# Later LayerNorm normalise behind a Newton pair, weight preparation after it, and residual loads moved to the end of the first gate/up pass

## The chip, the cores and the metric

The kernel runs on one core of one Trainium2 chip. The metric is the device time of an execution in microseconds (us); lower is better. Engines: PE is the matrix engine (PEld its weight loads), DVE the vector engine, ACT the scalar engine, POOL the GpSimd engine, SP the engine that only issues transfers here. All executions quoted are fast (mean granted matrix clock 0.990 to 1.000), and the ratios below compare times from the same chip and the same rounds; where medians of different rounds are set side by side, the text says so.

## The reference

```python
def reference(A_x, A_wqkv, A_wo, B_x, B_w_gate, B_w_up, B_w_down):
    x = A_x                                   # 1 x 2048 x 1024, bf16
    xn = _layernorm(x, axis=-1)               # eps 1e-5
    s = _A_ref(xn, A_wqkv, A_wo)              # linear attention, 32 heads of 32, phi = elu + 1
    g = _silu(_B_ref(xn, B_w_gate, B_w_up, B_w_down))   # silu(x Wg) * (x Wu), times Wd; F = 3584
    return x + s * g
```

So every token tile (128 tokens, 16 tiles) is normalised first, goes through the k/v projections and the k-v sums, later through q, the output projection and the large feed-forward part. At the end `x` and `s` are read again as residual inputs.

## The kernel before

Stage 1 handles 16 tiles `i` with four column pieces `c` each: `emit_Bmm` is 8 matmuls, `emit_Bev` evacuates them on ACT and DVE (`pk_sb` is DVE's result for pieces 0 and 1), and `emit_C(i-1)` adds the tile before to the k-v sums (`kvz`, needs `pk_sb`). Two pieces make a "half step". Behind this work the kernel prepares the statistics of tiles some steps ahead (`ln_pre`), normalises them (`emit_N`, whose result goes through a transposing transfer into `xnT`), and prepares feed-forward weights (`prep`: load, squared sum on ACT, scale on DVE, four subtractions on POOL, store).

```python
    PREP_AT = ((4, 3), (5, 3), (6, 1), (6, 3), (7, 3))
    # ... cut ...
    PRE_AT = {2: (5, 6), 3: (7, 8), 4: (9, 10), 5: (11, 12), 6: (13, 14), 7: (15,)}
    GRP = {5: (5, 6), 6: (5, 6), 7: (7, 8), 8: (7, 8), 9: (9, 10), 10: (9, 10), 11: (11, 12), 12: (11, 12),
           13: (13, 14), 14: (13, 14)}
    NR_ITERS = 3

    def emit_rstd(gid, eng=None):             # 1/sqrt(var + eps) of one or two tiles, by Newton's method
        eng = eng or nc.gpsimd
        mv, rstd, tiles = grp_state[gid]
        # ... cut: three small DVE instructions make the first guess y from a = var + eps ...
        for _ in range(NR_ITERS):
            eng.tensor_tensor(out=w[:, 0:n], in0=y, in1=y, op=ALU.mult)
            eng.tensor_tensor(out=w[:, 0:n], in0=w[:, 0:n], in1=a[:, 0:n], op=ALU.mult)
            eng.tensor_scalar(out=w[:, 0:n], in0=w[:, 0:n], scalar1=-0.5, scalar2=1.5, op0=ALU.mult, op1=ALU.add)
            eng.tensor_tensor(out=y, in0=y, in1=w[:, 0:n], op=ALU.mult)

    def ln_pre(i, eng=None):                  # statistics on DVE; Newton after the last tile of the group
        emit_stats(i)
        if i == grp_tiles(i)[-1]:
            emit_rstd(grp_of(i), eng)

    for i in range(2, NT):
        for c in range(NCH):
            # ... cut: statistics of wo and wv on ACT (so_stat), power-of-two scales ...
            if (i, c) != (2, 0):
                emit_Bmm(i, c)
            if c == 0:
                # ... cut ...
                emit_C(i - 1)
            emit_Bev(i, c)
            if (i, c) in PREP_AT:
                prep(1)
            if i >= 8 and c % 2 == 1:
                k = 2 * (i - 8) + c // 2
                prep(11 * (k + 1) // 16 - 11 * k // 16)
            if c % 2 == 1:
                for k in (PRE_AT[i - 1] if i - 1 in PRE_AT else (4,) if i == 2 else ())[c // 2:c // 2 + 1]:
                    emit_N(k)
                    # ... cut: loads of wo ...
                for k in PRE_AT.get(i, ())[c // 2:c // 2 + 1]:
                    ln_pre(k)
```

In the traces each engine's instructions start in the order written: in the kernel before, DVE stands 2.29 us for the normalise at 58.18 us, and the statistics written behind it start at 58.64. DVE meets, per tile: normalise, statistics, normalise, statistics, Newton's first guess, the phi work, and then the next normalise, which needs POOL's result of that Newton chain.

In the first of two gate/up passes (28 weight units, `n = 28`), some weights still arrive raw (`w_up`), and five pairs of residual tiles (128 KB of `x` and 128 KB of `s` each) are put on SP's issue queue. There the traces show one issue after the other: in the kernel before, one of `s` at 319.51 us takes 2.87 us, and the next one follows at 322.48. `io_load(mb)` makes each pair wait for the unit's matmul `mb`:

```python
                mb = emit_b(keys[i])
                if first and i in range(6, 11):
                    io_load(mb)
```

## Time and profile before

| | before |
|---|---|
| time, median of 4 executions | 765.71 us (764.83 to 766.57) |
| span of the profiled execution | 764.6 us |
| PE busy | 751.0 us (98%) |
| DVE, ACT, POOL busy | 73%, 49%, 36% |

Page of the kernel before: busy time of the engines, and the chain of work that ended last, by engine.

```profile
PE 751.0 (98%) x3731; PEld 349.3 (46%) x3731; DVE 556.3 (73%) x1043; ACT 376.2 (49%) x526; POOL 277.9 (36%) x340
...
PE 84%; DVE 6%; POOL 4%; DMA 3%; issue 2%; ACT 1%; SPq 0%; ACTq 0%; POOLq 0%
```

PE is nearly all of the span, but the chain that ended last is only 84% PE; the rest are stretches in which PE waited for something. Busy time in chosen 20-us stretches shows where: columns are the length, then busy us (instructions) of each engine, the granted clock, the share of the transfer engines and GB/s.

```profile
core 0: us, PE busy (x) PEld busy (x) DVE busy (x) ACT busy (x) POOL busy (x), PEclk, DMA share, GB/s
0.00:20.00 20.00, 17.33 (x84) 7.69 (x85) 14.31 (x53) 10.12 (x17) 0.80 (x9) 1.00 0.97 323
60.00:80.00 20.00, 17.18 (x99) 7.93 (x97) 15.03 (x43) 14.94 (x27) 8.04 (x27) 1.00 0.66 148
80.00:100.00 20.00, 17.93 (x111) 8.86 (x109) 15.86 (x35) 14.70 (x22) 19.09 (x22) 1.00 0.86 241
320.00:340.00 20.00, 18.65 (x89) 8.36 (x88) 15.10 (x28) 10.21 (x12) 10.23 (x12) 1.00 0.98 364
```

The start costs 2.7 us, stage 1 loses 2.8 and 2.1 us at 60 to 100 us, and 1.35 us are missing near 335 us. PE's waits name the releasers (total us, times, longest):

```profile
PE kvz L551 <- DVE pk_sb L163: 2.8, 4, 1.3
PE kv_ps L529 <- DVE pk_sb L163: 1.5, 1, 1.5
...
PE xb L940 <- ACT sg L1015: 1.2, 1, 1.2
PE kvz L551 <- ACT w_sb L260: 0.5, 1, 0.5
```

Now the chain of waits inside stage 1 (start us, duration, what). There is no PE in it: one turn leads from a normalise (L486) to the next one 8.93 us later.

```profile
49.25 0.55 DVE xn L486
49.80 1.21 DVE stats L448 x2
...
51.24 0.41 DVE xn L486
51.65 1.21 DVE stats L448 x2
...
53.12 0.18 DVE lna L470
...
54.15 0.73 POOL lnw L478
...
57.95 0.20 POOL rstd L481
58.18 0.55 DVE xn L486
```

DVE does two normalises, two statistics and the first guess, then POOL twelve operations on 128x2 elements (0.20 us each plus 0.07 us between them at best, up to 0.73 us for one, 4.4 us for all), and only then does the next normalise start. DVE stood 12.1 us for this in six waits between 36 and 95 us:

```profile
DVE xn L486 <- POOL rstd L481: 12.1, 6, 2.3
```

PE's own sequence in that time (start, duration, what, and in brackets the idle time just before and its releaser). The kvz groups come once per tile (in two halves of four where PE had to wait); the first two here are 7.36 us apart, the next 8.4, 8.9, 8.9:

```profile
48.06 0.63 PE L551 MATMUL kvz<-v_sb,pk_sb 128*128 128x129 bf16 x8
55.42 0.92 PE L551 MATMUL kvz<-v_sb,pk_sb 128*128 128x129 bf16 x8
...
63.80 0.40 PE L551 MATMUL kvz<-v_sb,pk_sb 128*128 128x129 bf16 x4 [0.55 <-DVE pk_sb L163]
...
72.72 0.40 PE L551 MATMUL kvz<-v_sb,pk_sb 128*128 128x129 bf16 x4 [0.32 <-DVE pk_sb L163]
...
81.59 0.39 PE L551 MATMUL kvz<-v_sb,pk_sb 128*128 128x129 bf16 x4
...
87.94 3.61 PE L529 MATMUL kv_ps<-wkv_sb,xnT 128*128 128x512 bf16 x16 [1.53 <-DVE pk_sb L163]
```

The stall near 335 us, in the chain of waits: a raw up-weight load issued at 317.05 lands 12.59 us later, ACT's work on it comes late, and PE waits for ACT.

```profile
317.05 12.59 DMA w_sb<-in_B_w_up_dram
...
332.32 1.89 ACT w_sb L1322
...
334.74 0.58 ACT sg L1015
...
335.36 1.02 PE xb L940 x4
```

### The profile page before, as it was taken

How to read it: one execution, taken by the hardware profiler on the slowest of the kernel's cores; microseconds unless marked ns; L12 is line 12 of the kernel's file. 1: busy time of each engine (PE TensorE's matmuls, PEld its weight loads, DVE VectorE, ACT ScalarE, POOL GpSimd, SP SyncE). 2: the span in 40 equal slices, each digit the busy share in tenths (PEclk: the TensorE clock that was granted, in tenths of full speed). 3: DMA queues.
4: the chain of work that ended last, by engine and by line, in shares of the span. 5: the costliest groups of instructions: out<-in, count | busy, mean ns of one | idle time of the engine just before them, and what ended most of it. 6: DMA issues, size and time to landing. Idle time of an engine off the chain costs nothing.

```text
span 764.6 us, 10494 instructions
## 1 busy us (share of the span) xinstructions
PE 751.0 (98%) x3731; PEld 349.3 (46%) x3731; DVE 556.3 (73%) x1043; ACT 376.2 (49%) x526; POOL 277.9 (36%) x340
## 2 busy tenths in 40 slices
PE   8998899999999999999999999999999999999997
PEld 3443444454444444444444444444444444444444
DVE  7767787888588788878889884458776767787335
ACT  4777666899865666566657411132323222211022
POOL 0443899998550255858686000110000000200000
PEclk9999999999999999999999999999999999999999
DMA  9966799959679669887889227398655444530824
GB/s 319 297 141 138 196 299 308 317 106 308 196 196 264 229 233 312 281 329 292 312 287 385 105 71 273 106 359 319 231 189 182 170 165 166 174 142 15 270 92 135
DMA packets 105845, 170.30 MB, mean 223 GB/s; under 512 B 34688, under 2 KB 82176, under 8 KB 95168
## 3 DMA queue, kind: packets, MB, share of 16 engines
q1 hardware_dynamic: 100144, 144.99, 58.5%
q0 software_dynamic: 4208, 22.15, 7.4%
q10 hardware_dynamic: 1440, 2.49, 1.1%
q8 instruction: 29, 0.48, 0.3%
q14 instruction: 24, 0.20, 0.1%
HBM read 111.67 MB, written 50.59 MB: 212 GB/s over the span
## 4 chain that ended last, share of the span: by engine, by line
PE 84%; DVE 6%; POOL 4%; DMA 3%; issue 2%; ACT 1%; SPq 0%; ACTq 0%; POOLq 0%
PE zw L940 23%; PE dzw L1125 12%; PE xb L940 12%; PE q_ps L183 7%; PE dx L1125 6%; PE yb L940 6%; PE kv_ps L529 6%; PE s_ps L749 3%; PE dy L1125 3%; PE fx L791 3%; DVE stats L448 2%; DMA w_sb<-in_B_w_up_dram 2%; POOL lnw L478 1%; DMA xp<-in_A_x_dram 1%; POOL rstd L481 1%
## 5 line engine op out<-in xcount | busy, mean ns | idle before, releaser
L940 PEld LDWEIGHTS <-w_sb 128*128 128x128 f16 (+1 forms) x1568 | 152.2, 98 | 184.4 <-issue 2.1
L529 PE MATMUL kv_ps<-wkv_sb,xnT 128*128 128x512 bf16 x512 | 113.9, 379 | 2.5 <-DVE pk_sb L163 1.5
L940 PE MATMUL xb<-xnT,w_sb 128*128 128x512 bf16 x448 | 115.0, 379 | 1.2 <-ACT sg L1015 1.2
L940 PE MATMUL zw<-xnT,w_sb 128*128 128x512 bf16 x448 | 105.8, 379 | 0.0
L940 PE MATMUL zw<-S,w_sb 128*128 128x512 f16 x448 | 105.8, 379 | 0.0
L295 POOL TENSOR_TENSOR w_sb<-w_sb 128x512 f16<-128x512 bf16 x42 | 50.6, 1204 | 94.3 <-DVE w_sb L283 51.6
L260 ACT ACTIVATE w_sb<-w_sb 128x2048 bf16<-128x2048 bf16 x42 | 79.9, 1902 | 9.6 <-DMA w_sb<-in_B_w_up_dram 9.6
L1125 PE MATMUL dx<-w_sb,hT 128*128 128x512 bf16 x210 | 79.6, 379 | 0.0
L529 PEld LDWEIGHTS <-xnT 128*128 128x128 bf16 x512 | 48.4, 98 | 58.5 <-issue 2.4
L1125 PEld LDWEIGHTS <-hT 128*128 128x128 bf16 (+1 forms) x462 | 45.2, 98 | 51.7
L183 PE MATMUL q_ps<-xnT,wq_sb 128*128 128x512 bf16 x256 | 58.4, 379 | 0.0
L1125 PE MATMUL dzw<-w_sb,hT 128*128 128x512 f16 x196 | 58.3, 379 | 0.0
L940 PE MATMUL yb<-S,w_sb 128*128 128x512 f16 x224 | 57.4, 378 | 0.0
L1016 ACT ACTIVATE sg<-cg 128x1024 bf16<-128x1024 f32 x28 | 29.6, 1057 | 56.4 <-DVE cg L1009 56.4
L1009 DVE SCALAR_TENSOR_TENSOR cg<-zw,rc_all,s 128x1024 f32<-128x1024 f32 x28 | 35.9, 1283 | 25.1 <-PE zw L940 14.0
L968 DVE SCALAR_TENSOR_TENSOR s<-yb,rc_all,s 128x512 f32<-128x512 f32 x42 | 31.5, 749 | 30.1 <-ACT s L967 30.1
L296 POOL TENSOR_TENSOR w_sb<-w_sb 128x512 f16<-128x512 bf16 x42 | 50.0, 1191 | 3.3
L298 POOL TENSOR_TENSOR w_sb<-w_sb 128x512 f16<-128x512 bf16 x42 | 50.7, 1208 | 0.0
L1065 POOL TENSOR_TENSOR hs<-hT 128x512 f16<-128x512 bf16 x2 | 2.5, 1252 | 132.6 <-ACT sg L1016 132.6
L297 POOL TENSOR_TENSOR w_sb<-w_sb 128x512 f16<-128x512 bf16 x42 | 50.3, 1199 | 0.0
L1099 POOL DMA_DIRECT2D out_dram<-io x16 | 8.7, 542 | 101.9 <-DVE io L1098 101.6
L967 ACT ACTIVATE s<-xb,rcl 128x512 f32<-128x512 f32 x14 | 9.6, 687 | 65.0 <-PE xb L940 65.0
(183 smaller groups left out, 1185.8 us busy)
## 6 DMA issues: line engine op xcount, KB each, us to landing
w_sb<-pk_g SPq DMA_DIRECT2D x27, 1024.0 KB, 5.7
pk_g<-w_sb SPq DMA_DIRECT2D x14, 1024.0 KB, 5.1
w_sb<-wd SPq DMA_DIRECT2D x14, 1024.0 KB, 5.4
w_sb<-pk_u SPq DMA_DIRECT2D x14, 1024.0 KB, 5.0
pk_u<-w_sb POOLq DMA_DIRECT2D x13, 1024.0 KB, 5.3
w_sb<-wd SPq DMA_DIRECT2D x14, 768.0 KB, 5.0
w_sb<-in_B_w_gate_dram SPq DMA_DIRECT2D x14, 512.0 KB, 5.5
w_sb<-in_B_w_down_dram SPq DMA_DIRECT2D x28, 256.0 KB, 5.0
```

The source lines that it names most:

```text
L183: nc.tensor.matmul(q_ps[:], lhsT=wq_sb[:, dc, g * P:(g + 1) * P], rhs=xn_ap(dc, btok), start=(dc == 0), stop=(dc == DC - 1))
L260: nc.scalar.activation(out=junk, in_=raw_view(key, t), func=ACT.Square, accum_out=asum[:])
L295: nc.gpsimd.tensor_tensor(out=T1, in0=b12, in1=b11, op=ALU.subtract)
L296: nc.gpsimd.tensor_tensor(out=T2, in0=b22, in1=T1, op=ALU.subtract)
L297: nc.gpsimd.tensor_tensor(out=T3, in0=b22, in1=b12, op=ALU.subtract)
L298: nc.gpsimd.tensor_tensor(out=T4, in0=b21, in1=T2, op=ALU.subtract)
L529: mm = nc.tensor.matmul(kv_ps[:], lhsT=xn_ap(dc, tok), rhs=wkv_sb[:, dc, c * CW:(c + 1) * CW], start=(dc == 0), stop=(dc == DC - 1))
L940: mm = nc.tensor.matmul(out, lhsT=lhs(k), rhs=rhs(k), start=(first and k == 0), stop=(k == HK - 1), skip_group_check=True)
L968: nc.vector.scalar_tensor_tensor(out=s2[:], in0=y_[:], scalar=rc, in1=s1[:], op0=ALU.mult, op1=ALU.add)
L1009: nc.vector.scalar_tensor_tensor(out=d12, in0=zw[:], scalar=rc, in1=s2[:, None, :].to_broadcast([P, 2, TB]), op0=ALU.mult, op1=ALU.add)
L1016: nc.scalar.activation(out=sg[:, 1:3, :], in_=cf[:], func=ACT.Silu)
L1125: nc.tensor.matmul(out, lhsT=lhs, rhs=rhs, start=first, stop=lastk, skip_group_check=True)
```

## The change

Its intent: each normalise of tiles 6 to 15 moves two half steps later, so that POOL's Newton result is ready when DVE gets there; the Newton pairs become (6,7), (8,9) ... (14,15), with tile 5 alone; weight preparation goes behind the normalise and loses one early slot, made up by 12 instead of 11 later; the residual loads go from units 6 to 10 to units 22 to 26 of the first pass.

```diff
-    PREP_AT = ((4, 3), (5, 3), (6, 1), (6, 3), (7, 3))
+    PREP_AT = ((4, 1), (5, 1), (6, 1), (7, 1))
@@
-        GRP = {5: (5, 6), 6: (5, 6), 7: (7, 8), 8: (7, 8), 9: (9, 10), 10: (9, 10), 11: (11, 12), 12: (11, 12),
-               13: (13, 14), 14: (13, 14)}
+        N_AT = {4: (4,), 6: (5,)}
+        for k in range(6, NT):
+            N_AT[k + 3] = (k,)
@@ def grp_tiles(gid):
-            return GRP.get(gid, (gid,))
+            return (gid,) if gid < 6 else (gid - gid % 2, gid - gid % 2 + 1)
@@ main loop of stage 1
                 emit_Bev(i, c)
-                if (i, c) in PREP_AT:
-                    prep(1)
-                if i >= 8 and c % 2 == 1:
-                    k = 2 * (i - 8) + c // 2
-                    prep(11 * (k + 1) // 16 - 11 * k // 16)
                 if c % 2 == 1:
-                    for k in (PRE_AT[i - 1] if i - 1 in PRE_AT else (4,) if i == 2 else ())[c // 2:c // 2 + 1]:
+                    for k in N_AT.get(2 * i + c // 2, ()):
                         emit_N(k)
                         # ... cut, unchanged ...
                     for k in PRE_AT.get(i, ())[c // 2:c // 2 + 1]:
                         ln_pre(k)
+                if (i, c) in PREP_AT:
+                    prep(1)
+                if i >= 8 and c % 2 == 1:
+                    k = 2 * (i - 8) + c // 2
+                    prep(12 * (k + 1) // 16 - 12 * k // 16)
@@ first gate/up pass
-                if first and i in range(6, 11):
+                if first and i in range(n - 6, n - 1):
                     io_load(mb)
```

## The prediction

> TensorE bounds the kernel: the page gives PE 751.0 of 764.6 us, so all its idle time is 13.6 us and no reordering can win over 1.8%. Busy time in 20-us stretches places it: 2.7 us at the start (untouched), 2.8 + 2.1 at 60 to 100 us, 0.5 near 223, 1.35 near 335, the rest at the end.
>
> **Stall 1, 60 to 88 us.** The table of waits shows PE waiting for DVE's pk_sb, 2.8 us in 4 waits before kvz and 1.5 once before kv_ps, and 0.5 for ACT. The chain of waits from 40 to 88 us has hardly any PE in it: DVE normalise (0.55), statistics of two tiles (2 x 1.2), Newton's head on DVE (0.6), twelve tiny POOL operations (4.4), the next normalise. One turn takes 8.93 us (49.25, 58.18, 67.09, 76.11), with DVE standing 2.3 us for POOL's last rstd; a tile costs PE about 7.4 us (32 matmuls 216 ns apart, kvz 0.46). This loop, not PE, paces tiles 4 to 8; until 60 us a backlog hides it.
>
> The change breaks the loop: the pair's Newton is started two or three half steps (over 7 us) ahead of the normalise, against 4.4 us of POOL. No operation is added: nine Newton chains before and after (tile 5 alone, 14 and 15 paired). Without the wait DVE has about 6.6 us per tile, under PE's 7.4. The 1.53 us at 86 us goes too: DVE waited there for tile 15's own Newton, then normalised in 1.35 instead of 0.55 us while POOL ran. [...] Transposes stay about 11 us ahead of their tile's first matmul, against 3.2 us to landing.
>
> Against it: preparation moves later, its squares onto tiles 7 to 9. There ACT has an estimated 7.7, 7.7 and 8.8 us per tile (2.1 per square, 1.25 per wo or wv square, 0.5 per piece) against PE's 7.4, so 0.3 to 1.5 us of stall may stay. POOL's T work starts one preparation later in program order, but near 79 us instead of 83.6, since DVE no longer lags; relative to PE nothing shifts. Gain: 4.9 less about 0.7, 4.2 us.
>
> **Stall 2, near 334 us.** The chain shows a raw w_up load issued at 317.05 landing after 12.59 us (median 5.4), then ACT's work on it, and PE waiting 1.2 us for ACT's sg. The issue queue interleaves five pairs of residual loads (256 KB each) between 295 and 322 us, with DMA about full; one holds the queue for 2.87 us. Moving them to units 22 to 26 (about 450 to 490 us, DMA share 0.3 to 0.7) takes 0.5 MB out of the way there, an estimated 1.5 us at the 350 GB/s seen, and the issue comes a microsecond earlier. Gain: 1.2 us. They are needed only after 515 us.
>
> Sum: 5.4 us off 766.55, so **761.2 us**; 80% range 758.5 to 765.0. Faster by over 2%: 1%; within 2%: 98%; slower by over 2%: 1%.
>
> **Right if:** PE busy stays near 751 and its idle time at 60 to 100 us is below 1.5 us; DVE no longer waits for POOL's rstd; the 8.93-us turn becomes about 7.4; that w_up load lands within 9 us and PE has no wait near 330.
>
> **Wrong if:** ACT on tiles 7 to 9 becomes the limit and gives back over 2 us; stores behind POOL hold the in-order issue queue, so that oT transposes near 150 us come late; another raw load stalls PE instead; late residual loads delay weight tiles of the first down pass.

## The result, and the profile after

The changed kernel takes 759.22 us (median of 4 executions, 759.13 to 759.30) against 765.71 us (764.83 to 766.57). The ratio is 0.9915, 95% interval 0.9898 to 0.9932; a ratio here is the mean time of one kernel's fast runs over that of the other's of the same rounds, so not quite the ratio of the medians. It is correct, and lies within 2% of before.

Page of the changed kernel, and its busy time in the three stretches that had lost time, columns as before (the lines of the file are one higher). This trace lacks 69 of PE's 3731 matmul records, so its PE busy time is too low by a few us, and full stretches read 19.89 instead of 20.00.

```profile
PE 746.2 (99%) x3662; PEld 349.2 (46%) x3731; DVE 559.9 (74%) x1043; ACT 375.7 (50%) x526; POOL 276.8 (37%) x340
...
PE 94%; DVE 2%; DMA 1%; ACT 1%; issue 1%; SPq 0%; ACTq 0%; DVEq 0%
```

```profile
60.00:80.00 20.00, 19.89 (x117) 9.92 (x118) 14.27 (x38) 16.56 (x30) 9.49 (x26) 1.00 0.77 133
80.00:100.00 20.00, 19.89 (x115) 9.74 (x116) 16.93 (x35) 15.52 (x23) 17.25 (x15) 1.00 0.84 277
320.00:340.00 20.00, 19.89 (x96) 9.10 (x97) 16.56 (x26) 11.38 (x15) 12.46 (x13) 1.00 0.83 294
```

The chain that ended last is now 94% PE, and the three stretches at 60 to 100 and at 320 to 340 us are full. PE's waits in the changed kernel (those left out are 0.4 us or less): neither pk_sb nor the feed-forward's sg is in the list.

```profile
PE warm_ps L566 <- DVE warm L563: 1.5, 1, 1.5
PE fx L792 <- DVE wq_sb L785: 0.5, 1, 0.5
...
PE nd L264 <- ACT w_sb L260: 0.3, 1, 0.3
```

DVE's wait for POOL's rstd between 36 and 95 us, 12.1 us before, is:

```profile
DVE xn L487 <- POOL rstd L482: 0.9, 1, 0.9
```

and PE's kvz groups stay 7.36 to 7.57 us apart (the first four of them):

```profile
48.12 0.63 PE L552 MATMUL kvz<-v_sb,pk_sb 128*128 128x129 bf16 x8
...
55.49 0.62 PE L552 MATMUL kvz<-v_sb,pk_sb 128*128 128x129 bf16 x8
...
62.85 0.62 PE L552 MATMUL kvz<-v_sb,pk_sb 128*128 128x129 bf16 x8
...
70.42 0.62 PE L552 MATMUL kvz<-v_sb,pk_sb 128*128 128x129 bf16 x8
```

Landmarks of the two traces (first matmul into q_ps, into the first zw, into the first dx, end of span; kvz of tile 4 is the common start, at 48.06 and 48.12 us) show where the 7.1 us of the two spans come from:

| stretch | before | after | difference |
|---|---|---|---|
| kvz of tile 4 to first q_ps (rest of stage 1) | 86.2 | 80.1 | -6.1 |
| first q_ps to first zw (stage 2) | 117.9 | 118.5 | +0.6 |
| first zw to first dx (first gate/up pass) | 169.7 | 168.0 | -1.7 |
| first dx to the end | 342.7 | 342.8 | +0.1 |

The up-weight load of the second stall, in the list of transfers issued between 308.5 and 318.5 us (count, size, us from issue to landing), before and then after:

```profile
w_sb<-in_B_w_up_dram SPq DMA_DIRECT2D x1, 512.0 KB, 12.6
```

```profile
w_sb<-in_B_w_up_dram SPq DMA_DIRECT2D x1, 512.0 KB, 6.9
```

### The profile page after: what moved, and what is told of

Same layout as the page of the kernel before. It is cut to its first block, busy times and chain, and to the rows that moved or that the text cites. A ratio compares the mean times of both kernels' runs of the same rounds, so it can differ in the third digit from the quotient of the medians.

```text
span 757.5 us, 10426 instructions
## 1 busy us (share of the span) xinstructions
PE 746.2 (99%) x3662; PEld 349.2 (46%) x3731; DVE 559.9 (74%) x1043; ACT 375.7 (50%) x526; POOL 276.8 (37%) x340
## 4 chain that ended last, share of the span: by engine, by line
PE 94%; DVE 2%; DMA 1%; ACT 1%; issue 1%; SPq 0%; ACTq 0%; DVEq 0%
PE zw L941 26%; PE kv_ps L530 13%; PE xb L941 13%; PE dzw L1126 12%; PE yb L941 6%; PE q_ps L183 6%; PE dx L1126 6%; PE dy L1126 3%; PE fx L792 3%; PE s_ps L750 2%; DMA xp<-in_A_x_dram 1%; PE kvz L552 1%; PE nd L719 1%; PE df L1126 1%; DVE w_sb L283 0%
## 5 line engine op out<-in xcount | busy, mean ns | idle before, releaser
L941 PE MATMUL xb<-xnT,w_sb 128*128 128x512 bf16 x420 | 113.3, 379 | 1.5
L1126 PE MATMUL dx<-w_sb,hT 128*128 128x512 bf16 x202 | 76.6, 379 | 0.3
L1126 PE MATMUL dzw<-w_sb,hT 128*128 128x512 f16 (+1 forms) x190 | 57.0, 379 | 0.0
L968 ACT ACTIVATE s<-xb,rcl 128x512 f32<-128x512 f32 x14 | 9.6, 687 | 65.3 <-PE xb L941 65.3
```

The costliest lines, as they stand in the source:

```text
L941: mm = nc.tensor.matmul(out, lhsT=lhs(k), rhs=rhs(k), start=(first and k == 0), stop=(k == HK - 1), skip_group_check=True)
L1126: nc.tensor.matmul(out, lhsT=lhs, rhs=rhs, start=first, stop=lastk, skip_group_check=True)
```

## The experiments

Theory A says that the DVE-POOL loop of Newton's method paced tiles 5 to 9. Rival B says that the gain came from moving preparation work away from these tiles. For the second stall, theory C says that the residual loads' bytes and places in the issue queue made a raw up-weight load late; rival D says that its lateness is a matter of how transfers happen to fall.

| run | time us (median) | runs | before | ratio (95%) |
|---|---|---|---|---|
| e1_norm | 759.32 | 4 | 765.32 | 0.9918 (0.9906 to 0.9931) |
| e2_prep | 765.19 | 5 | 765.32 | 0.9996 (0.9984 to 1.0008) |
| e3_io | 764.65 | 5 | 765.32 | 0.9991 (0.9978 to 1.0004) |
| e4_newton1 | 759.54 | 6 | 765.32 | 0.9926 (0.9913 to 0.9939) |
| e5_newton5 | 785.97 | 4 | 764.96 | 1.0276 (1.0261 to 1.0291) |
| e6_after_newton5 | 766.34 | 4 | 764.96 | 1.0017 (1.0000 to 1.0034) |
| e9_dummy1 | 759.92 | 4 | 764.96 | 0.9935 (0.9920 to 0.9950) |
| e9_dummy3 | 764.32 | 4 | 764.96 | 0.9993 (0.9971 to 1.0015) |
| e12_after | 759.20 | 5 | 765.94 | 0.9918 (0.9904 to 0.9931) |
| e8_k2 | 759.24 | 4 | 765.94 | 0.9916 (0.9903 to 0.9930) |
| e11_newton2 | 760.17 | 5 | 765.94 | 0.9924 (0.9912 to 0.9937) |
| e10_swap | 759.01 | 4 | 765.94 | 0.9914 (0.9901 to 0.9928) |

All twelve gave correct results.

### The parts alone

**e1_norm**: the kernel before with only the new groups and the later normalise.

```diff
-        GRP = {5: (5, 6), ...}
+        N_AT = {4: (4,), 6: (5,)}  # and N_AT[k + 3] = (k,) for k from 6
-            return GRP.get(gid, (gid,))
+            return (gid,) if gid < 6 else (gid - gid % 2, gid - gid % 2 + 1)
-                    for k in (PRE_AT[i - 1] ...)[c // 2:c // 2 + 1]:
+                    for k in N_AT.get(2 * i + c // 2, ()):
```

> Only the later normalise and the new Newton pairs; weight preparation and residual loads as before. Theory A (tiles 4 to 8 were paced by DVE standing for POOL's Newton): the first q_ps matmul comes at 128 to 129.5 us instead of 134.3, no PE wait for pk_sb is left at 60 to 88 us, and the time is 759.5 to 761.5 us, with the PE wait near 330 us still there in the executions that have it. Rival B (the gain came from moving preparation work away from tiles 4 to 7): first q_ps at 133 or later and a time above 764 us.

Measured: 759.32 us, first q_ps at 128.5 us, no PE wait for pk_sb, and of DVE's 12.1 us of waits this is left:

```profile
DVE xn L487 <- POOL rstd L482: 0.9, 1, 0.9
```

This part alone gives the whole gain; it changes the pairs and the places of the normalise together, and their shares were not separated. Contrary to the expectation, its profile shows no wait near 330 us, although the residual loads are where they were; its four times (759.10 to 759.43) lie too close together for two groups.

**e2_prep**: only the new `PREP_AT`, the preparation behind the normalise, and 12 for 11.

> Only the preparation moved (four early slots, behind the normalise, twelve later); normalise and residual loads as before. Theory A: within 1 us of before, first q_ps at 133.5 to 135, the 8.93-us turn of DVE and POOL unchanged. Rival B: 4 to 6 us faster, first q_ps at 128 to 130.

Measured: 765.19 us, no change; DVE still waits 12.9 us for rstd and PE 2.8 us for pk_sb ahead of kvz. Its first q_ps is 1.2 us earlier (133.1), a little more than expected, but first q_ps to first zw takes 119.4 us instead of 117.9 (PE waits 1.0 us there for DVE's pqT), so it is given back. Rival B falls.

**e3_io**: only the last hunk of the diff.

> Only the residual loads moved. Theory C (their bytes and their places in the issue queue made one raw up-weight load land late): the PE wait near 334 us is gone, first q_ps stays at 134.3, the first dx matmul comes at 420 to 420.5 instead of 421.9, and the time is 764.7 to 765.0 us in all executions, so about 0.9 us under the mean of before, which has two modes (764.85 and 766.55). Rival D (that late landing is a matter of how DMA traffic happens to fall, whatever the residual loads do): two modes and the same mean as before, or the wait moves to another up-weight load.

Measured: 764.65 us against 765.32, with an interval that includes no change. The profile is as theory C has it: the load lands after 7.6 us, PE has no wait near 334 us, and the first dx comes at 419.8 us. All five times lie between 764.43 and 765.16, where before has 764.61 to 767.33 in eleven. But before has executions as fast as these, so this run alone does not rule out rival D.

### The dose of the chain

**e4_newton1, e11_newton2, e5_newton5**: the kernel before, nothing reordered, one line changed.

```diff
-        NR_ITERS = 3
+        NR_ITERS = 1        # e4; 2 in e11, 5 in e5
```

> The kernel before with one Newton iteration instead of three in every LayerNorm chain of POOL (4 POOL operations instead of 12; rstd less exact, perhaps up to 0.2%, on purpose); nothing is reordered. Theory A: the chain shrinks from 4.4 to about 1.5 us, which is more than the 2.3 us DVE stood, so DVE no longer waits for POOL and most of the gain of the first part comes without any reordering: first q_ps at 128 to 130 us, time 759.5 to 762 us. Rival B: no change above 1 us.

> The kernel before with two Newton iterations instead of three, nothing reordered. The turn was 8.93 us with three and 11.1 with five, so two make an estimated 7.8 against PE's 7.37; over about five turns that is 2 us, of which the backlog hides most: 759.3 to 761.5 us. Rival B: as before, above 764 us.

> The kernel before with five Newton iterations instead of three (20 POOL operations instead of 12, about 1.1 us per added iteration); results are as exact or better. Theory A: each turn of the DVE-POOL loop grows by 2.2 us from 8.93 to about 11.1, over about six turns with no backlog left to hide it: first q_ps near 146 to 149 us, time 776 to 781 us. Rival B: under 2 us slower.

| iterations | kvz of tile 4 to first q_ps, us | DVE's wait for rstd, 36 to 95 us | time us |
|---|---|---|---|
| 1 | 80.8 | none listed | 759.54 |
| 2 | 80.1 | 4.3 | 760.17 |
| 3 (before) | 86.2 | 12.1 | 765.3 to 765.9 |
| 5 | 101.0 | 25.6 | 785.97 |

The runs with one, two and five iterations are from three different calls. The time follows the length of the chain, with a threshold: at two iterations or fewer PE sets the pace, above that the loop does. With five, kvz groups came 11.1 us apart, as estimated. The total was missed by 5 us. The early tiles suffer too: tile 4's kvz comes at 53.88 us instead of 48.06, 5.8 us late. These are PE's waits in the run with five iterations:

```profile
PE kvz L551 <- DVE pk_sb L163: 9.6, 7, 2.8
PE kv_ps L529 <- DVE pk_sb L163: 3.7, 1, 3.7
PE tr_ps L513 <- DVE xn L486: 3.3, 2, 1.7
```

(tr_ps is the transposition of the first four tiles.) This run is also not a dose of the chain alone: its mean granted clock is 0.991 (the kernel before: 0.999 or 1.000 in the same call), and PE's matmuls come slower in three places. 32 of kv_ps from 66.33 us on take 8.75 us (7.07 from 55.19), 24 from 89.37 take 7.87 (5.34 from 77.65), and 16 from 106.88 take 5.30 (3.61 from 114.43); some groups lack one record. That the clock fell in these places is inferred from both. After each of the first two PE waits for the loop again; in the third, and from there to the first q_ps, PE has no such wait, so it costs an estimated 1.7 us (5.30 less 3.61) of the 101.0 us. Shortening the chain by one iteration, with correct results, gives nearly the same gain as the reordering; the rest of the difference, 760.17 to 759.20, has the size of the second stall, which that run's profile does show; see below.

**e6_after_newton5**: the changed kernel with five iterations.

> The changed kernel with five Newton iterations instead of three. Theory A: the normalise comes about 11 us behind the start of its chain, which now takes about 6.6 us, so the added 8 operations cost nothing: 759.0 to 760.0 us, no PE wait for pk_sb. If the distance were only just enough, 762 us or more.

Measured: 766.34 us, so the expectation was missed by 6 us. Where it was lost:

```profile
PE tr_ps L514 <- DVE xn L487: 2.1, 2, 1.8
PE kv_ps L530 <- DMA xnT<-xn: 2.0, 2, 1.1
...
PE q_ps L183 <- DVE pqT L151: 1.0, 1, 1.0
```

The change leaves the normalise of tiles up to 5 close behind their own chains, so DVE stood for these, and the chain of tiles 6 and 7 started late as well; PE waited for the transposes of tiles 5 and 6. The mean granted clock of this execution was 0.997 instead of the changed kernel's 0.999, an estimated 1.5 us more (0.2% of 764.7 us). From the kvz of tile 6 on, to the first q_ps, both kernels take 65.3 us (69.00 to 134.3 here, 62.85 to 128.2 in the changed kernel): for the later tiles of stage 1 eight more operations per chain cost PE nothing. Theory A holds for them; my expectation had forgotten that the early tiles have no such distance. The wait of q_ps lies in stage 2, which takes 119.7 us here; what made pqT late there was not tested.

**e8_k2**: one half step less distance.

```diff
-            N_AT[k + 3] = (k,)
+            N_AT[k + 2] = (k,)
```

> The changed kernel with the normalise two half steps behind the statistics index (k+2) instead of three, so one half step, about 3.7 us, less distance; the pair's chain still has at least 7 us. Theory A (a distance above the chain's 4.4 us plus 0.6 us is all that is needed): within 0.4 us of the changed kernel, no PE wait for pk_sb. If more distance were needed: 760.5 us or more.

Measured: 759.24 us against 759.20 for the changed kernel in the same rounds. DVE's wait for rstd is 3.2 us instead of 0.9, but PE has none for pk_sb. One half step would have done.

**e12_after**: the changed kernel, unedited, as reference of these rounds.

> The changed kernel again, unedited, as the reference for the other runs of these rounds: 759.1 to 759.4 us.

Measured: 759.20 us (758.94 to 759.45).

### The residual loads

**e9_dummy1 and e9_dummy3**: the changed kernel with extra copies in the old places.

```diff
@@ cut: dm_d, ten (thirty in e9_dummy3) otherwise unused buffers in HBM
+                if first and i in range(6, 11):
+                    for q in range(1):        # 3 in e9_dummy3
+                        gate([nc.sync.dma_start(out=dm_d.pop()[:], in_=src[i * P:(i + 1) * P, 0:CW])
+                              for src in (x2, s_dram)], mb, sync=True)
                 if first and i in range(n - 6, n - 1):
                     io_load(mb)
```

> The changed kernel with extra copies in the places where the residual loads were before (units 6 to 10 of the first pass): five pairs of 128 KB copies from the same rows into an unused HBM buffer, so the same bytes read, and written to HBM instead of the chip's buffer. Theory C (bytes and queue places delay the raw up-weight load): it lands 10 to 11 us after its issue near 311 us instead of 6.9, as in the run with only the normalise moved (10.8); the time stays 759.2 to 760.8 us, since up to about 11 us are covered. Rival D: lands after about 7 us.

> As the run with one extra set, with three sets of copies. Theory C: the up-weight load lands after 14 us or more, PE waits near 330 us for ACT behind it, and the time is 762 us or more. Rival D: no change above 0.5 us against the changed kernel.

Measured with one set: issue at 311.97, landing after 8.9 us, between the two expectations (6.9 and 10 to 11), time 759.92 us (759.59 to 760.41), no PE wait. With three sets: 764.32 us (762.78 to 766.29). The lateness took another shape than expected: the watched load was issued only at 317.82 us instead of 309.62, behind the copies, and then needed just 5.7 us, while an earlier up-weight load took 12.25 us. PE waited twice for the work behind them. Theory C's direction is shown, by these two runs with the landings below. Whether bytes or queue places weigh more was not separated.

These are PE's instructions of e9_dummy3 around the waits, and then two stretches, 318 to 326 us, where the number after POOL's is PE's granted clock:

```profile
317.00 0.16 PE L264 MATMUL yb<-asum,ones 128*128 128x1 bf16 x1 [1.86 <-DVE s L969]
...
320.59 1.87 PE L941 MATMUL xb<-xnT,w_sb 128*128 128x512 bf16 x4 [2.54 <-ACT sg L1016]
322.25 3.30 PE L941 MATMUL zw<-S,w_sb 128*128 128x512 f16 x8
...
326.24 1.89 PE L941 MATMUL zw<-xnT,w_sb 128*128 128x512 bf16 x8
```

```profile
318.00:321.00 3.00, 0.47 (x3) 0.13 (x2) 2.84 (x7) 3.00 (x5) 3.00 (x4) 0.54 1.04 362
321.00:326.00 5.00, 5.00 (x15) 1.83 (x14) 1.42 (x4) 3.17 (x4) 4.91 (x6) 0.59 1.06 376
```

The granted clock is 1.00 from 314 to 318 us, 0.54 and 0.59 in these two stretches, and 1.00 from 326 to 330 us. If it was either full or half, 0.54 and 0.59 put the half from about 318.2 to 325.1 us, by estimate: it falls after the wait of 1.86 us, at the start of that of 2.54 us, and stays so for some 7 us. 8 matmuls take 3.30 us instead of 1.89. So two waits of 4.4 us, 4.7 us by start-to-start distances, cost 6.9 us in this trace (first zw to first dx 174.9 instead of 168.0 us); about 2.2 us of it is the lower clock. The four executions differ by it: those with a mean clock of 0.995 and 0.996 took 766.29 and 765.61 us, those with 0.999 and 1.000 took 763.03 and 762.78.

The landing of the same load over the runs: 6.8 to 7.6 us in three without early residual loads (e12_after, after, e3_io); 9.7, 10.7 and 10.8 in e2_prep, e4_newton1 and e1_norm, with them and without a PE wait; 12.1 and 12.6 in e11_newton2 and before, with a PE wait of 1.2 us in both. So early residual loads go with 2 to 6 us more, and PE notices from somewhere between 10.8 and 12.1 us. Rival D keeps a part: why the load lands after 9.7 us in one kernel and 12.6 in another, with the residual loads in the same places, stays open. In the last call, four executions of before lie at 764.62 to 764.78 and five at 765.94 to 766.48; the two-iteration kernel has 758.86 and 759.01, and 760.17 to 760.51 in three. The changed kernel's five lie within 758.94 to 759.45. That the upper group is the executions with this wait fits its size, but only the profiled executions show it directly.

### A further version

**e10_swap**: the changed kernel, one more edit at PE's wait of 0.5 us for DVE's sums (the fx line of the waits).

```diff
-        u["w"]()
-        emit_S(1, 3, 1, fx[4])
+        emit_S(1, 3, 1, fx[2])
+        u["w"]()
```

> The changed kernel with one more edit at the other stall left in the trace (PE waits 0.48 us for DVE's sums near 218 us): the last plain output product of block 1 is issued before the first product that needs the sums, in an accumulator that is free at that time. If that stall is on the critical path: 0.4 to 0.5 us below the changed kernel of the same rounds, 758.6 to 758.9 us; else equal.

Measured: 759.01 us (758.80 to 759.25) against 759.20 (758.94 to 759.45). The wait is gone from the trace, and first q_ps to first zw takes 118.3 instead of 118.6 us. The times overlap, so it is not shown to be faster than the changed kernel.

## Why the prediction was right or wrong

The time, 759.22 us, lies in the range 758.5 to 765.0, below the centre of 761.2; the mechanism of both stalls was right. The centre was 5.4 us off 766.55, the median of the three executions of before then known (764.83, 766.55 and 766.57); the fourth took 764.88. Off 766.55 the gain is 7.3 us.

- **The loop paces tiles.** Right: shown by e1_norm, and by the dose of one, two, three and five iterations. "DVE no longer waits for POOL's rstd" held (12.1 to 0.9 us), and so did the turn of about 7.4.
- **"Gain: 4.9 less about 0.7, 4.2 us."** This is the term that was mis-sized. It measured 6.1 us in the traces, 5.5 after the 0.6 us that stage 2 lost. (The medians of e1_norm's rounds are 6.0 us apart, but in some executions of before they also hold the second stall.) Both of its parts were off. The 4.9 was PE's idle time as the profile counts it. The trace lists a matmul of 512 columns at 379 ns, but in a stream the matmuls start 216 ns apart (8 in 1.73 us). So, by an estimate from these two, each record reaches 163 ns past the time when the next matmul could have started, and every stall in the list looks 163 ns shorter than it is. Six stalls make 1.0 us; a seventh, at 55.4 us (kvz 0.92 instead of 0.62), never showed as idle. Start-to-start distances show all of it: from the kvz at 55.42 to that at 91.39 us it is 35.97 us in before, the same four steps after (55.49 to 85.25 us) 29.76, a difference of 6.2. The deducted 0.7 us, ACT on tiles 7 to 9 falling behind, did not come: kvz groups there are 7.4 to 7.6 us apart. ACT had less to do than estimated. 7.7, 7.7 and 8.8 us of work would have kept it busy throughout these three tiles; in the changed kernel, between the kvz groups at 62.85, 70.42, 77.81 and 85.25 us, it is busy for 6.1, 6.2 and 7.4 us and idle for 2.6, and in the tile after for 4.6 of 7.6 us, so nothing was left over that could add up. Instead 0.6 us went in stage 2. About half of it is PE's wait for ACT's squared sum (the nd line of the waits), which every run of the changed kernel lists, and before, e1_norm, e3_io, e4_newton1 and e11_newton2 do not, so it came with the moved preparation. The other half, 0.5 us in e1_norm, is two waits too short for the list, which before does not have, both for DVE: in e1_norm DVE ends a pqT at 146.86 us and PE's nd group goes on at 146.92 (0.90 us for the group instead of 0.64), and DVE ends its reading of nd at 150.58 and the next group begins at 150.64. What makes DVE late there was not tested.
- **"Gain: 1.2 us" for the second stall.** The stall went (1.7 us between landmarks), and the load landed in 6.9 us. But it is hardly in every execution of before, whose times fall into two groups, so its worth is less: 0.67 us between medians for e3_io, not separated from zero, and nothing visible on top of e1_norm (759.32 alone, 759.20 with everything, in different calls). I took one profiled execution for all of them.
- **"About 450 to 490 us, DMA share 0.3 to 0.7"** and **"They are needed only after 515 us"** were wrong. A unit lasts 6.0 us (168.0 us for 28), not the 9 that these times imply, so the loads were issued at 387 to 411 us, where the transfer engines are full, as this stretch of the changed kernel shows:

```profile
385.00:415.00 30.00, 29.84 (x140) 13.59 (x141) 27.00 (x45) 20.50 (x21) 20.55 (x20) 1.00 1.02 381
```

  Their first use is at 443 us. It did no harm: PE has no wait there, and the same stretch was just as full before (1.01 at 392 to 422 us).
- **Preparation and POOL.** "Relative to PE nothing shifts" held to 0.6 us: no store behind POOL delayed an oT transpose enough to make PE wait.
- **The normalise of 1.35 us at 83.6 us** (0.49 to 0.55 us for the six before it) ran beside a POOL subtraction of 1.15 us (from 83.56). After the change the normalises in that stretch are listed at 0.54 or 0.55 us, but here a shorter wait and less overlap came together, so no run shows what made it long.

## What to carry to other kernels

When one engine needs a tiny result from another, look at the distance in program order between producer and consumer, not at the busy shares: here DVE at 73% and POOL at 36% formed a loop that paced an engine at 98%. Either put more work between them than the chain takes (the wait fell from 12.1 to 0.9 us), or shorten the chain; one Newton iteration less did nearly as much as the reordering. Size a stall by start-to-start distances of PE against an undisturbed stretch, not by the idle time between its records (6.2 against 4.9 us here), and look at several executions before counting a stall that hangs on when a transfer lands. Look at the granted clock too, before putting all of a lost time down to a wait (about 2.2 of 6.9 us in e9_dummy3).
